# The closing rows of a gated mixer kernel: one fused scale moved to the end, one sum moved to a DMA, the order of the last operations rewritten

## The chip, the cores and the metric

The kernel runs on one core of one Trainium2 chip. The time is device microseconds of one execution; runs are given by their median. "The profile" is one execution taken by the hardware profiler, and its span runs from its first to its last instruction. The engines are PE (matmuls), ACT (ScalarE), DVE (VectorE), POOL (GpSimd) and SP (SyncE, which here only issues transfers).

## The reference

Two branches work on the same input `x = A_q` (2048 tokens of 640 values), and a gate mixes them. Branch A multiplies a shifted, weighted `k` with `v`, convolves the result along the tokens with a 2048-tap filter per channel (by Fourier transforms), adds `kv * ssm_D` and multiplies with `q`. Branch B is a layer norm, a product with `w1`, gelu, a shift of channel groups along the tokens, a product with `w2`, a residual, a second layer norm and an MLP with 1536 hidden values.

```python
x = A_q
g = _sigmoid((x * gate_w).sum(-1, keepdims=True))
...
kv = k_shift * v
y_f = kv_f * kf_f[None, :, :, :]
y = irfft2(y_f, ...)[:, 0, :S, :]
y = y + kv * ssm_D[None, None, :]
a = q * y
...
x1 = x + hs
b = x1 + _gelu(_layernorm(x1) @ w3) @ w4
return g * a + (1 - g) * b
```

## The kernel before

All tiles lie in one SBUF tensor, `arena`, and all accumulators in one PSUM tensor, `PS`, used as four pairs of banks. Tokens are split into two halves of the sequence (`c` = 0, 1), each half into 128 partitions of eight neighbours; "row" `rho` (0 to 7) is one of the eight, so that a row is 2 x 128 tokens. Channels are worked on in two halves of 320 (`half` = 0, 1).

The tile `X` first holds the input, then branch B's running result; branch B ends by leaving `(1 - g) * b` in it. Branch A runs over each half of the channels: forward transforms of the taps `h` and of `kv` by matmuls (L1178; evicted from PSUM by ACT at L694), twiddles and pointwise products on DVE (L663, a helper that issues every elementwise operation), and an inverse transform by matmuls in `inverse` (L1366 and L1341). The taps of one half give two spectra, one for each of two interleaved sets of frequencies, evicted to the slots `s3` and `s4`; the DVE work on `s3` is first.

`inverse` goes over the rows in the order `INV` = 0, 4, 2, 6, 1, 5, 3, 7. Of the second half of the channels (`half` 1), which ends the kernel, the rows 0, 4, 2 and 6 are worked whole: 8 matmuls (L1366), two ACT evictions that scale by the gate `g` (320 wide, one for each `c`), a DVE multiply with `q` (640 wide) and a DVE add into `X` (640 wide), and an output transfer of 160 KB issued by SP (L1400). The rows 1, 5, 3 and 7, at the places 4 to 7 of `INV`, are cut into pieces "a" (`c` = 0) and "b" (`c` = 1), so that "6b" is the second half of the row at place 6: 4 matmuls (L1341), one eviction, a DVE multiply and a DVE add of 320. Both pieces of a row go out in one transfer (L1359), those of place 7 each in its own (80 KB, L1356). One piece, 7b, has no ACT eviction: one DVE operation reads PSUM and does scale and multiply (L1351).

In `half` 0 a DVE multiply writes the product over `q`, and a DMA issued by POOL (L1392, queue q0) adds it into `X`; there are four such sums, each of two rows (320 KB), and SP issues the outputs behind them.

The program is recorded as nodes with costs. A planner (`_forward`) then sets each engine's order: among the nodes that are ready it takes the one that can start first by its own estimates, and the table `RANK` (one number for a node) breaks ties. It also gives out the PSUM pairs. Each engine then runs its list in that order and waits on semaphores. SP's list is such a queue too: a transfer that waits holds all that stand behind it.

Of the kernel before, what the change touches and what calls it, by code (L numbers as in the profile page):

```python
# [4 lines left out]
ENGS = ("pe", "act", "dve", "pool", "sp")  # L5
# [83 lines left out]
class Prog:  # L89
# [110 lines left out]
    def _forward(self):  # L200
# [6 lines left out]
            j.pair = None  # L207
            j.left = len(j.evicts) if j.evicts else 1
        free = {"pe": 1.0, "act": 0.7, "dve": 0.8, "pool": 1.1, "sp": 0.7}
        ready = {e: [] for e in ENGS}  # L210
        known_at = {}
        pair_free = [0.0] * PAIRS
        pair_job = [None] * PAIRS
# [11 lines left out]
        def arrive(n):  # L225
            at = 0.0
            for d in n.deps:
                t = d.end + (LAT[d.eng][0 if d.eng == n.eng else 1] if d.kind == "c" else 0.05)
                if t > at:
                    at = t  # L230
            known_at[n] = at
            ready[n.eng].append(n)

        for n in nodes:
            if n.missing == 0:
# [4 lines left out]
        while left:  # L240
            best = None
            for e in ENGS:
                for n in ready[e]:
                    t = max(known_at[n], free[e])
                    if n.first:
                        j = n.job
                        tp = None
                        for i in range(PAIRS):
                            if pair_job[i] is not None and pair_job[i].left:
                                continue  # L250
                            if j.seeded and not (bits[i][0] and bits[i][1]):
                                continue
                            if tp is None or pair_free[i] < tp:
                                tp = pair_free[i]
                        if tp is None:
                            continue
                        t = max(t, tp)
                        ok = True
                        for d in j.ext:
                            if d.end is None:  # L260
                                ok = False
                                break
                            if not n.seed:
                                t = max(t, d.end - n.cost)
                        if ok and n.seed:
                            for d in n.soft:
                                if d.end is None:
                                    ok = False
                                    break
                                t = max(t, d.end - self.LOOK)  # L270
                        if not ok:
                            continue
                    key = (t, -n.prio, n.idx)
                    if best is None or key < best[0]:
                        best = (key, n)
            assert best is not None, "schedule is stuck"
            n = best[1]
            e = n.eng
            t = best[0][0]
            ready[e].remove(n)  # L280
            n.start = t
            cost = n.cost
            if n.array:
# [153 lines left out]
def _bf16_bits(a):  # L437
# [21 lines left out]
XQ = {(0, 0): "act", (0, 1): "act"}  # L459
FIN2 = {0: 4, 1: 0}  # L460
FIN_DMA = (0,)
FIN1_DMA = 0
SEED2 = (0, 1, 2, 3, 4, 5, 6, 7)
SEED4 = (0, 1, 2, 3, 4, 5, 6, 7)
RANK = [
# [40 lines left out]
]  # L506


# [42 lines left out]
def bass_gated_mix__ssm_conv_h3__mixer_s_mlp__prompt_kernel(  # L551
# [761 lines left out]
    def inverse(half, slot0, slot1, Qh, temp):  # L1313
# [8 lines left out]
        for rho in order:  # L1322
# [63 lines left out]
                sel = slice(rho, rho + 1)  # L1386
            xs = X[:, :, sel, hs]
            n = 1280 if pair else 640
            if half in FIN_DMA or (half == 1 and order.index(rho) // 2 < FIN1_DMA):
                qs = Qh[:, :, sel, :]  # L1390
                tt(qs, g2, qs, ALU.mult, n, tag="fin")
                P.dma("pool", lambda e, ps, xs=xs, qs=qs: e.dma_start(xs, qs, accum_op=ALU.add), r=[xs, qs], w=[xs],  # L1392
# [57 lines left out]
```

## Time and profile before

| | |
|---|---|
| three runs | 225.64, 225.78, 226.91 us; median 225.78 us |
| the profiled execution | 225.55 us, its span 223.5 us |
| busy in the span | PE 216.3 us, DVE 208.7, ACT 174.6, POOL 41.1 |
| transfers | 34.04 MB, mean 152 GB/s |
| clock granted to PE | 0.998 of full speed |

The span is shorter than the time of its execution by 2.05 us, which lie around it. PE's busy time is 97% of the span, so there is little slack in the middle; what the change rewrites lies in the last 12 us.

### The profile page before, as it was taken

The numbers are of one execution on the slowest core, as the hardware profiler recorded it, in microseconds if no ns is written. First come the engines' busy times: TensorE is split into PE (matmuls) and PEld (weight loads), VectorE is DVE, ScalarE is ACT, GpSimd is POOL, SyncE is SP. The second block draws the span as 40 slices with busy tenths as digits, with TensorE's granted clock in tenths as the row PEclk, the third lists the DMA queues.
The fourth block names the chain that finished last, engine by engine and source line by source line (L and its number), as shares of the span: only waits on it lengthen the run. The fifth ranks groups of instructions, "written<-read, shape, count | busy, mean of one in ns | idle before, by whom it ended". The sixth has DMA issues, their size and how long they took to land.

```text
span 223.5 us, 3945 instructions
## 1 busy us (share of the span) xinstructions
PE 216.3 (97%) x1557; PEld 138.0 (62%) x1569; DVE 208.7 (93%) x267; ACT 174.6 (78%) x292; POOL 41.1 (18%) x48
## 2 busy tenths in 40 slices
PE   7999999999999999999999999999999999999993
PEld 7589655557676655457744455667745675577772
DVE  4999899999999899999899999799998999999976
ACT  3989999899999999999987488997145723572484
POOL 1335662403003120450200200000020002033020
PEclk9999999999999999999999999999999999999999
DMA  6999996589801968061654150003559000648667
GB/s 208 385 403 387 350 361 236 116 156 283 349 5 33 345 120 337 4 117 41 126 101 90 24 97 0 1 3 98 137 87 257 11 0 3 117 87 117 151 117 235
DMA packets 36713, 34.04 MB, mean 152 GB/s; under 512 B 17508, under 2 KB 31719, under 8 KB 36568
## 3 DMA queue, kind: packets, MB, share of 16 engines
q1 hardware_dynamic: 31560, 23.97, 35.8%
q0 software_dynamic: 4848, 9.50, 18.9%
q10 hardware_dynamic: 288, 0.33, 0.6%
q8 instruction: 12, 0.20, 0.4%
q14 instruction: 5, 0.04, 0.1%
HBM read 21.47 MB, written 3.93 MB: 114 GB/s over the span
## 4 chain that ended last, share of the span: by engine, by line
PE 76%; ACT 18%; DVE 2%; DMA 2%; issue 1%; SPq 0%; ACTq 0%
PE PS L1147 23%; PE PS L1129 23%; ACT arena L694 12%; PE PS L1178 9%; PE PS L967 8%; PE PS L1366 6%; ACT PS L1057 5%; PE PS L927 2%; ACT arena L680 2%; DVE arena L663 2%; DMA arena<-in_A_q_dram 2%; PE PS L823 1%; PE PS L769 1%; PE PS L758 1%; PE PS L780 0%
## 5 line engine op out<-in xcount | busy, mean ns | idle before, releaser
L663 DVE TENSOR_TENSOR arena<-arena 128x2560 bf16<-128x2560 bf16 (+5 forms) x175 | 186.1, 1116 | 7.0 <-ACT arena L694 3.5
L694 ACT ACTIVATE arena<-PS 128x640 bf16<-128x640 f32 (+8 forms) x142 | 104.2, 812 | 18.9 <-PE PS L1129 14.7
L1147 PE MATMUL PS<-arena 128*128 128x320 bf16 x384 | 53.3, 299 | 0.0
L1129 PE MATMUL PS<-arena 128*128 128x512 bf16 x232 | 52.2, 379 | 0.8 <-ACT arena L694 0.5
L1147 PEld LDWEIGHTS PS<-arena 128*128 128x128 bf16 x384 | 37.4, 98 | 15.0 <-issue 0.3
L694 ACT ACTIVATE arena<-PS,arena 128x320 bf16<-128x320 f32 (+1 forms) x47 | 27.7, 626 | 24.2 <-PE PS L1147 22.2
L1129 PEld LDWEIGHTS PS<-arena 128*128 128x128 bf16 x240 | 23.3, 98 | 27.4 <-issue 0.5
L1178 PE MATMUL PS<-arena 128*128 128x320 bf16 x224 | 34.4, 300 | 0.7 <-DVE arena L906 0.6
L1178 PEld LDWEIGHTS PS<-arena 128*128 128x128 bf16 x224 | 20.8, 98 | 12.8 <-ACT arena L694 2.8
L680 ACT ACTIVATE arena<-arena 128x640 bf16<-128x640 bf16 (+2 forms) x34 | 25.8, 787 | 0.8 <-DMA arena<-in_A_q_dram 0.4
L967 PE MATMUL PS<-arena 128*128 128x512 bf16 (+1 forms) x121 | 22.9, 335 | 0.2
L1075 PE MATMUL PS<-arena 128*128 128x320 bf16 x160 | 22.6, 299 | 0.0
L1057 ACT ACTIVATE PS<-arena 128x640 f32<-128x640 bf16 x32 | 22.3, 719 | 0.2
L868 POOL TENSOR_TENSOR arena<-arena 128x4 f32<-128x4 f32 (+1 forms) x9 | 14.0, 1553 | 30.7 <-DVE arena L668 30.4
L1075 PEld LDWEIGHTS PS<-arena 128*128 128x128 bf16 x160 | 15.4, 98 | 6.7 <-ACT PS L1057 0.6
L967 PEld LDWEIGHTS PS<-arena 128*128 128x128 bf16 x125 | 11.8, 98 | 8.2 <-ACT arena L694 0.5
L702 POOL DMA_DIRECT2D arena<-arena x4 | 4.8, 1202 | 57.6 <-DVE arena L663 57.6
L888 DVE BATCH_NORM_STATS2 arena<-arena 128x6 f32<-128x320 bf16 x28 | 12.4, 477 | 2.9 <-DMA arena<-in_A_q_dram 2.8
L1366 PE MATMUL PS<-arena 128*128 128x320 bf16 x96 | 14.3, 299 | 0.0
L1007 POOL DMA_DIRECT2D arena<-arena x18 | 9.7, 545 | 12.7 <-ACT arena L694 12.7
L1366 PEld LDWEIGHTS PS<-arena 128*128 128x128 bf16 x96 | 9.2, 98 | 4.3 <-issue 0.3
L1392 POOL DMA_DIRECT2D arena<-arena x4 | 5.1, 1276 | 35.7 <-ACT arena L694 25.9
(42 smaller groups left out, 81.5 us busy)
## 6 DMA issues: line engine op xcount, KB each, us to landing
arena<-in_B_w_dram POOLq DMA_DIRECT2D x4, 960.0 KB, 8.2
arena<-in_A_k_dram SPq DMA_DIRECT2D x4, 640.0 KB, 14.3
arena<-in_A_v_dram SPq DMA_DIRECT2D x4, 640.0 KB, 14.1
arena<-arena POOLq DMA_DIRECT2D x4, 640.0 KB, 6.1
arena<-in_A_q_dram SPq DMA_DIRECT2D x4, 640.0 KB, 7.4
out_dram<-arena SPq DMA_DIRECT2D x15, 160.0 KB, 2.0
arena<-in_A_q_dram SPq DMA_DIRECT2D x6, 320.0 KB, 5.5
arena<-in_A_ssm_k_dram SPq DMA_DIRECT2D x3, 512.0 KB, 11.5
```

What stands on the lines that cost most here:

```text
L663: return dve(lambda e: e.tensor_tensor(o, a, b, op), [a, b], [o], c_tt(n), tag=tag, **kw)
L680: node = P.op("act", lambda e, ps: e.activation(o, i, func, **kw), r=r, w=[o], cost=c_act(n, naps, acc is not None, psum=False), tag=tag, ...
L694: node = P.op("act", lambda e, ps: e.activation(ov, inner(ps), func, **kw), r=r, w=[o], cost=c_act(n, len(r), acc is not None), job=job, t ...
L868: P.op("pool", lambda e, ps: e.tensor_tensor(r, v, hv, ALU.pow), r=[v, HALF], w=[r], cost=cost, tag="ln")
L888: dve(lambda e, o=o, x=x: e.bn_stats(o, x), [x], [o], 0.393, tag="bn", group=("bn", id(mv), rho, c))
L967: fns.append(lambda e, ps, b=b, c=c, lhsT=lhsT: e.matmul(bank(ps, b, 256 * n), lhsT, XT[:, c, r0:r0 + n, :], start=(c == 0), stop=(c == 4)))
L1057: P.seed(job, lambda e, ps: e.activation(two(ps, 320), x, ACTF.Copy), [X[:, c, rho, :]], c_act(640, psum=False), tag)
L1075: fns.append(lambda e, ps, hh=hh, ft=ft, lhsT=lhsT: e.matmul(bank(ps, hh, 320), lhsT, w2v[:, ft, 320 * hh:320 * hh + 320], start=False, st ...
L1129: fns.append(lambda e, ps, b=b, ft=ft, c=c, sc=sc: e.matmul(bank(ps, b, 512), w3h[ft // 6][:, c, 128 * (ft % 6):128 * (ft % 6) + 128], XT[ ...
L1147: fns.append(lambda e, ps, hh=hh, ft=ft, lhsT=lhsT: e.matmul(bank(ps, hh, 320), lhsT, w4h[ft // 6][:, ft % 6, 320 * hh:320 * hh + 320], st ...
L1178: fns.append(lambda e, ps, w=w, b=b, rhs=rhs, st=(first and n == 0), en=(n == len(ss) - 1): e.matmul(bank(ps, b, 320), w, rhs, start=st, s ...
L1366: fns.append(lambda e, ps, w=w, z=z, c=c, st=(n == 0), en=(n == len(terms) - 1): e.matmul(bank(ps, c, 320), w, z[:, c, :], start=st, stop=en))
```

## The change

Three things change in what is executed. (1) Row 6 of the second half is no longer added into `X` by DVE: the multiply writes over `q`, and a DMA on POOL's queue adds it, as in the first half. Its output, which stood first of its half in SP's queue, now stands behind those of the places 4 and 6. (2) Piece 7b, whose matmuls stood before those of row 4, is now the last on PE, its fused DVE operation and its output transfer likewise; the DVE operations of the closing pieces now alternate between the add of one piece and the multiply of another. (3) In the forward transforms of the taps of the second half, the last matmuls and eviction for `s3` change places with the next-to-last for `s4`. The planner now follows `RANK` strictly, one list an engine, instead of picking among ready nodes; the table has new numbers.

```diff
-        ready = {e: [] for e in ENGS}
+        queue = {e: sorted((n for n in nodes if n.eng == e), key=lambda n: -n.prio) for e in ENGS}
...
-            ready[n.eng].append(n)
...
-                for n in ready[e]:
+                n = queue[e][len(order[e])] if len(order[e]) < len(queue[e]) else None
+                if n in known_at:
...
-            ready[e].remove(n)
...
-FIN1_DMA = 0
+FIN1_ROWS = (6,)
...
 RANK = [
-    920, 917, 905, 923, 915, 904, 888, 870, 898, 848, 853, 801, 812, 918, 877, 913, 779, 795, 738, 866, 753, 716, 721,
+    920, 917, 905, 923, 915, 904, 889, 871, 899, 853, 858, 804, 815, 918, 877, 914, 781, 798, 741, 866, 756, 720, 724,
...
-            if half in FIN_DMA or (half == 1 and order.index(rho) // 2 < FIN1_DMA):
+            if half in FIN_DMA or (half == 1 and rho in FIN1_ROWS):
                 qs = Qh[:, :, sel, :]
                 tt(qs, g2, qs, ALU.mult, n, tag="fin")
                 P.dma("pool", lambda e, ps, xs=xs, qs=qs: e.dma_start(xs, qs, accum_op=ALU.add), r=[xs, qs], w=[xs],
                       nbytes=256 * n, cost=1.3, kind="acc", tag="fina")
```

From line 281 on, the lines of the changed kernel stand one lower: L1366 is its L1365, L663 its L662. The first place is PE's last instructions. Before, the last four rows of the list are row 4's neighbours and pieces: L1366 x24 are the rows 6, 2 and 0, L1341 x4 is piece 7b, L1366 x8 is row 4, and L1341 x28 are the seven other pieces.

```order
L1366 MATMUL PS<-arena 128x320 x16
L1147 MATMUL PS<-arena 128x320 x24
L1366 MATMUL PS<-arena 128x320 x24
L1341 MATMUL PS<-arena 128x320 x4
L1366 MATMUL PS<-arena 128x320 x8
L1341 MATMUL PS<-arena 128x320 x28
```

Changed:

```order
L1365 MATMUL PS<-arena 128x320 x16
L1146 MATMUL PS<-arena 128x320 x24
L1365 MATMUL PS<-arena 128x320 x32
L1340 MATMUL PS<-arena 128x320 x32
L1419 UNCONDITIONAL_BRANCH
```

Row 4 now follows row 0 at once, and all eight pieces stand behind it, 7b last. The number of matmuls is the same.

The second place is DVE's end. A row of 640 in one run (128x640) is a multiply of a whole row, 128x2x320 an add of a whole row into `X`, 128x320 an operation of a piece. Before:

```order
L663 TENSOR_TENSOR arena<-arena 128x640
L663 TENSOR_TENSOR arena<-arena 128x2x320
L663 TENSOR_TENSOR arena<-arena 128x640
L663 TENSOR_TENSOR arena<-arena 128x2x320
L1351 SCALAR_TENSOR_TENSOR arena<-PS,arena 128x320
L663 TENSOR_TENSOR arena<-arena 128x640
L663 TENSOR_TENSOR arena<-arena 128x320
L663 TENSOR_TENSOR arena<-arena 128x2x320
L663 TENSOR_TENSOR arena<-arena 128x640
L663 TENSOR_TENSOR arena<-arena 128x320
L663 TENSOR_TENSOR arena<-arena 128x2x320
L663 TENSOR_TENSOR arena<-arena 128x320 x13
```

Changed:

```order
L662 TENSOR_TENSOR arena<-arena 128x2x320
L662 TENSOR_TENSOR arena<-arena 128x640
L662 TENSOR_TENSOR arena<-arena 128x2x320
L662 TENSOR_TENSOR arena<-arena 128x640
L662 TENSOR_TENSOR arena<-arena 128x2x320
L662 TENSOR_TENSOR arena<-arena 128x640
L662 TENSOR_TENSOR arena<-arena 128x320
L662 TENSOR_TENSOR arena<-arena 128x2x320
L662 TENSOR_TENSOR arena<-arena 128x320 x12
L1350 SCALAR_TENSOR_TENSOR arena<-PS,arena 128x320
L662 TENSOR_TENSOR arena<-arena 128x320 x2
```

The first row here is row 6's multiply, which now writes over `q` (hence its other shape). Its add is gone; the fused operation of 7b and its add have moved to the end, the fused one between the multiply and the add of 7a.

The third place is SP's queue of outputs: L1400 are whole rows, L1359 the rows at the places 4, 6 and 5, L1356 the pieces 7b and 7a. Before:

```order
L1400 DMA out_dram<-arena 128x2x320 x9
L1356 DMA out_dram<-arena 128x320
L1400 DMA out_dram<-arena 128x2x320 x3
L1359 DMA out_dram<-arena 128x2x320 x3
L1356 DMA out_dram<-arena 128x320
```

Changed:

```order
L1399 DMA out_dram<-arena 128x2x320 x11
L1358 DMA out_dram<-arena 128x2x320 x2
L1399 DMA out_dram<-arena 128x2x320
L1358 DMA out_dram<-arena 128x2x320
L1355 DMA out_dram<-arena 128x320 x2
```

The L1399 between the L1358 is row 6's output, which waits for its sum by DMA. POOL's list has one more transfer at its end (L1391, 128x2x320), that sum, behind the last sum of the first half.

76 rows, old and new, of the table RANK are left out of this document.

## The prediction

> **What bounds the kernel now.** I read the page first, then the chain of waits over the last 19 us, then the timeline of each engine there, then the transfers.
>
> ```profile
> PE 216.3 (97%) x1557; PEld 138.0 (62%) x1569; DVE 208.7 (93%) x267; ACT 174.6 (78%) x292; POOL 41.1 (18%) x48
> PE 76%; ACT 18%; DVE 2%; DMA 2%; issue 1%; SPq 0%; ACTq 0%
> ```
>
> PE is the bound: 216.3 us busy in a span of 223.5, and 76% of the chain. DVE is busy for 93% but is 2% of the chain, so most of what it gains or loses is absorbed. The change leaves PE's work as it is, so what counts is what comes after the last matmul. The end of the chain (start, length, what):
>
> ```profile
> 211.10 3.26 PE PS L1366 x24
> 214.37 0.54 PE PS L1341 x4
> 214.91 1.10 PE PS L1366 x8
> ...
> 216.03 0.95 ACT arena L694 x2
> 216.99 0.02 issue
> 217.01 3.98 DVE arena L663 x15
> ...
> 221.02 0.33 DVE arena L663
> ```
>
> PE carries the chain to 216.01 (the rows 6, 2, 0, then piece 7b, then row 4), two ACT evictions of row 4 to 216.98, and then DVE, without a pause, to 221.35. Behind it stands only the last output. The same stretch by engine (idle before the group in brackets):
>
> ```profile
> 212.48 1.26 POOL L1392 DMA_DIRECT2D arena<-arena  x1 [7.42 <-DVE arena L663]
> 213.37 1.95 DVE L663 TENSOR_TENSOR arena<-arena 128x640 bf16<-128x640 bf16 x4 [1.18 <-ACT arena L694]
> ...
> 215.23 0.54 DVE L1351 SCALAR_TENSOR_TENSOR arena<-PS,arena 128x320 bf16<-128x320 f32 x1
> 215.69 1.12 DVE L663 TENSOR_TENSOR arena<-arena 128x640 bf16<-128x640 bf16 x3
> ...
> 215.83 3.97 PE L1341 MATMUL PS<-arena 128*128 128x320 bf16 x28
> 216.03 4.33 ACT L694 ACTIVATE arena<-PS,arena 128x320 bf16<-128x320 f32 x9 [0.68 <-PE PS L1366]
> 217.01 4.33 DVE L663 TENSOR_TENSOR arena<-arena 128x640 bf16<-128x640 bf16 x16 [0.20 <-ACT arena L694]
> ```
>
> PE ends at 219.80, ACT at 220.36, DVE at 221.34. Before 217.01 DVE waits for ACT (1.18 and 0.20 us); after it DVE is the bound. SP's queue, from the release of the last DMA sum of the first half on:
>
> ```profile
> 217.05 0.37 SPq L1400 DMA_DIRECT2D out_dram<-arena  x1
> 217.47 0.47 SPq L1356 DMA_DIRECT2D out_dram<-arena  x1
> 217.99 1.51 SPq L1400 DMA_DIRECT2D out_dram<-arena  x3
> 219.54 1.61 SPq L1359 DMA_DIRECT2D out_dram<-arena  x3
> 221.37 0.34 SPq L1356 DMA_DIRECT2D out_dram<-arena  x1
> ```
>
> Nine outputs go out here, the first five steps at (219.54 - 217.05) / 5 = 0.50 us each. These do not wait for data: DVE had finished with the rows and with 7b some tenths or more before each. So SP is within a hair of being the bound as well; only the last issues wait for DVE. The windows (length, busy time of PE, PEld, DVE, ACT, POOL with counts, clock, share of the DMA engines, GB/s) say the same of the transfers:
>
> ```profile
> 214.30:216.50 2.20, 2.20 (x18) 1.57 (x17) 2.17 (x7) 1.42 (x4) 0.00 (x0) 1.00 1.22 149
> 216.50:217.50 1.00, 1.00 (x10) 0.72 (x8) 0.80 (x3) 1.00 (x4) 0.00 (x0) 1.00 1.07 322
> 217.50:218.00 0.50, 0.50 (x5) 0.35 (x4) 0.50 (x3) 0.50 (x2) 0.00 (x0) 1.00 0.09 28
> 218.00:219.00 1.00, 1.00 (x10) 0.73 (x8) 1.00 (x5) 0.92 (x3) 0.00 (x0) 1.00 0.78 245
> 219.00:222.50 3.50, 0.80 (x6) 0.35 (x4) 2.31 (x10) 1.35 (x3) 0.00 (x0) 1.00 0.97 300
> ```
>
> From 219.0 to 222.5 the DMA engines are full. Three things thus end within some tenths of each other: DVE's list, SP's list and the transfers.
>
> **The change part by part.** *PE, 0.* The matmuls are the same. Row 4 moves up by the 4 matmuls of 7b, 0.54 us, and ends at 216.01 - 0.54 = 215.47; the list still ends at 219.80, now with 7b. A wait for a PSUM pair could open a gap, but each pair's eviction lies at least 0.4 us ahead of the matmuls that take it.
>
> *ACT, 0.* The same operations. Row 4's second eviction ends at 216.98 - 0.54 = 216.44; each later piece comes 0.54 us earlier with its matmuls, 7a's ending near 219.8. None is last.
>
> *DVE, +0.05.* Row 6's add leaves (a whole-row operation), but it ran before 217.01, where DVE waits for ACT anyway: worth nothing at the end. The closing run starts 0.54 earlier, at 216.47. It takes in what 7b did before it:
>
> ```profile
> 219.02 0.79 DVE L663 TENSOR_TENSOR arena<-arena 128x320 bf16<-128x320 bf16 x3
> ```
>
> Three operations of 320 in 0.79, each 0.32 long, start every 0.24. The fused one at 215.23 is followed at 215.69: 0.46. So 0.46 + 0.24 = 0.70 is added. Alternating takes out the one pause left, between 7a's multiply and its add (0.32 + 0.04 instead of 0.24): -0.12. The run ends at 216.47 + 4.33 + 0.70 - 0.12 = 221.38, against 221.34. 7b moved from a place where DVE had time to one where it has none, and that eats the earlier start.
>
> *POOL and the sum by DMA, 0 if it lands by 220.1.* The issue stands behind the one at 212.48 (free at 213.75) and behind row 6's multiply (213.37 + 0.49). I take 214.3 to leave POOL half a microsecond. Nearest landings, from issue, in us (KB each before it):
>
> ```profile
> arena<-arena POOLq DMA_DIRECT2D x1, 320.0 KB, 4.6
> arena<-arena POOLq DMA_DIRECT2D x1, 320.0 KB, 6.3
> arena<-arena POOLq DMA_DIRECT2D x1, 640.0 KB, 6.6
> ```
>
> The first is the one at 212.48, the second that of 203.79, the third a pointwise sum at 163.36. The 320 KB hold the DMA engines for 2.2 us (the window 214.30 to 216.50), so these 160 KB hold them for 1.1, behind the others: 216.5 to 217.6, landing about 218.1. Bounds: 218.1 and 214.3 + 6.6 = 220.9. Those 1.1 us fall into the window 216.5 to 217.5, from which row 6's output (some 0.5 us) leaves; the gap at 217.5 to 218.0 takes the rest.
>
> *SP, +0.25.* This is where I expect the change to show. Row 6's output leaves the idle time at 214.4 and joins the crowd: ten outputs from 217.05 on instead of nine. At 0.50 a step the tenth starts at 217.05 + 9 x 0.50 = 221.55; the ninth (7a) waits for its add until 221.18, and one step more gives 221.68. I take 221.65, against 221.37 now, although 7b's data are there at 221.42. Bounds: 221.42 (SP keeps up; +0.05) and 221.68 plus 0.2 if a step in the full queue stretches (+0.5). The transfers agree: eight outputs of 160 KB at 0.53 and two of 80 KB from 218.0 on end near 222.8, now near 222.5.
>
> *The last landing, +0.05.* 80 KB take, from issue:
>
> ```profile
> out_dram<-arena SPq DMA_DIRECT2D x1, 80.0 KB, 1.6
> out_dram<-arena SPq DMA_DIRECT2D x1, 80.0 KB, 1.7
> ```
>
> 1.6 is the last one now, 1.7 the one inside the crowd (217.47). The new last one stands right behind another: between the two. Bounds 0 and +0.1.
>
> *The exchanged evictions, 0.* DVE waits in the middle for the last eviction of the taps' first spectrum:
>
> ```profile
> 143.63 1.49 DVE L663 TENSOR_TENSOR arena<-arena 128x2560 bf16<-128x2560 bf16 x1 [1.65 <-ACT arena L694]
> ```
>
> The evictions around it, by line and shape, and then all that PE waits for from 140 us to the end:
>
> ```profile
> L694 ACT ACTIVATE arena<-PS 128x640 bf16<-128x640 f32 x7 | 4.3, 735 | 0.0
> ```
>
> ```profile
> PEld PS L1178 <- ACT arena L694: 0.6, 3, 0.2
> PEld PS L1366 <- issue: 0.3, 1, 0.3
> PEld PS L1366 <- ACT arena L694: 0.2, 1, 0.2
> ```
>
> That eviction, one of a run of seven, now comes one place earlier, 4.3 / 7 = 0.6 us, so DVE starts its work on the second half 0.6 earlier. But PE does not wait for DVE in that time, and DVE's lead is lost at the 1.18 us wait at 213.37. If that cover were gone it would be worth up to -0.6.
>
> *Sum:* 0 + 0 + SP's 0.25 to 0.3 (DVE's 0.05 lies inside it) + 0.05 = **+0.3 us**: span 223.8, this execution 225.55 to 225.85. The median of the runs lies 0.23 above the profiled execution, so I forecast 225.78 + 0.3 = 226.1. A measurement of this kernel tells about 1% (2.3 us) from no change, so this is "the same".
>
> **The rivals.** *A late sum holds SP's queue (slower).* The outputs of place 5, 7a and 7b stand behind row 6's output, which waits for the sum. It decides from 220.1 on, when SP comes to it: each 0.1 later is 0.1 more. Landing after 6.6 us means 220.9, last issue 222.5, +0.85 over the forecast: 227.0. For it: two of the three rows above took over 6 us. Against: the 6.3 fell into outputs already moving beside it, and the nearest in place and time took 4.6 at twice the bytes. To be slower by 1% it would have to land 7.7 us after its issue.
>
> The Trainium skill speaks for this rival (SBUF — State Buffer, "SBUF: two separate sides"): while DVE runs an operation in a two-port mode, GpSimd is locked out of the shared ports and cannot write the descriptors of its DMAs. By that rule the issue would stretch while DVE works. The rows do not bear it out:
>
> ```profile
> 199.36 2.96 DVE L663 TENSOR_TENSOR arena<-arena 128x1280 bf16<-128x1280 bf16 x3
> 200.48 1.28 POOL L1392 DMA_DIRECT2D arena<-arena  x1 [2.37 <-DVE arena L663]
> ```
>
> With DVE busy throughout, the issue took 1.28; at 212.48, with DVE idle up to 213.37, 1.26. Had the descriptors to wait for the end of DVE's run at 221.38, the sum would land 4.6 - 1.26 = 3.3 later, at 224.7, and the last output would start 1.5 after that: 4.5 us more than forecast, 230.6. I give that 0.02 of this rival's 0.10.
>
> *The close is free.* SP steps faster than 0.50 when the queue of data, not of issues, is the limit, and 7b goes out at 221.42: +0.05, 225.8. For it: an issue with nothing before it takes 0.37. Against: six steps in a row at 0.5.
>
> *The exchange pays.* DVE's 0.6 reaches the end through some transfer that starts earlier: 226.1 - 0.6 = 225.5. Against: the sum that SP waits for until 217.05 is issued behind an ACT eviction that PE paces, not behind DVE.
>
> **How the numbers follow.** Forecast 0.68, free close 0.14, exchange 0.08, late sum 0.10. Run to run the times spread by 0.14 us below and 1.13 above their median, and the bounds of SP's term are +0.05 and +0.5; with the exchange below and the late sum above, the range is 225.5 to 227.0. Faster by over 1% has no case (0.02 for what I have not seen); slower by over 1% needs a landing beyond 7.7 us (0.04); the same 0.94.
>
> **What would show it.** PE's last matmul ends near 219.8 and DVE's closing run starts near 216.5, ending near 221.4: else the DVE term is wrong. SP issues ten outputs from 217.05 on, the last near 221.65: if it issues at 221.4, SP's step is wrong. Row 6's sum lands near 218.1; if SP waits for POOL's DMA after 220, the late sum is right. DVE's wait near 143 shrinks from 1.65 to about 1.05 with nothing else moving. The forecast is wrong if the span ends below 223.4 or above 224.6.

## The result: 0.2 to 0.4% longer, and the profile after

Before, 225.9 us (median of 20 runs beside the changed kernel); after, 226.72 us (226.13 to 228.54, 20 runs). The ratio is 1.0036 [1.0020, 1.0053]: about 0.8 us longer, clear of no change by its interval, and a third of the 1% that the prediction counts as the same. Measured again beside the experiments, the unaltered changed kernel took 226.4 us against 226.12: 1.0022 [0.9992, 1.0052], which does not exclude no change. The ratios leave out the few executions that were over 1.5% longer (of the profiled ones only that of the kernel with row 4 by DMA, span 228.3 us, granted clock 0.978), and are not always the quotient of the two medians.

The first profiled execution of the changed kernel took 227.75 us with a span of 225.5, 2 us longer than before's. Most of that is not the change. From the page:

```profile
PE 216.9 (96%) x1557; PEld 137.7 (61%) x1569; DVE 208.5 (92%) x266; ACT 174.8 (78%) x292; POOL 42.4 (19%) x49
L1365 PE MATMUL PS<-arena 128*128 128x320 bf16 x96 | 14.2, 299 | 0.6 <-DVE arena L662 0.6
```

DVE has one operation less and POOL one more, as the change says. The second row shows a wait of PE for DVE, 0.6 us, that before did not have. It stands at 212.40. Earlier in this execution the pointwise sum of the middle landed 8.1 us after its issue, and DVE waited 2.11 us for it; before, it landed after 6.6, and DVE waited 0.62. The rows of this transfer, of after and then of the second profile of the same kernel:

```profile
arena<-arena POOLq DMA_DIRECT2D x1, 640.0 KB, 8.1
```

```profile
arena<-arena POOLq DMA_DIRECT2D x1, 640.0 KB, 6.7
```

With 6.7 the second profile has no such wait of PE. How far an execution is set back ahead of the end is read from single matmuls. From the 801st to the end of the last one PE took 118.62 us before, 118.62 in the second profile of the changed kernel, and 118.62 or 118.63 in all the experiments below; only the first profile has 119.34. What else differs between executions lies ahead of the 801st matmul, which started between 101.1 and 105.6 us after the span's start, in kernels whose engines' lists are the same there. So single spans cannot be compared to tenths here, and everything below is counted **from the end of PE's last matmul** (219.80 before; 216.74 + 4.51 = 221.25 after). The chain of after near its end:

```profile
213.91 3.00 PE PS L1365 x22
216.92 0.02 issue
216.94 0.96 ACT arena L693 x2
217.90 0.02 issue
217.92 3.97 DVE arena L662 x15
```

Row 4 now goes straight from PE (216.92) over two evictions to DVE's closing run at 217.92, 3.33 us ahead of PE's end; before, it was 219.80 - 217.01 = 2.79. The groups of PE and of DVE, with the fused operation of 7b (L1350) inside the run and no pause around it:

```profile
216.74 4.51 PE L1340 MATMUL PS<-arena 128*128 128x320 bf16 x32
215.75 6.14 DVE L662 TENSOR_TENSOR arena<-arena 128x640 bf16<-128x640 bf16 x19 [0.42 <-ACT arena L693]
221.81 0.55 DVE L1350 SCALAR_TENSOR_TENSOR arena<-PS,arena 128x320 bf16<-128x320 f32 x1
222.27 0.55 DVE L662 TENSOR_TENSOR arena<-arena 128x320 bf16<-128x320 bf16 x2
```

DVE ends at 222.82, 1.57 after PE; before 1.54. What comes later is SP's queue. Its rows in the second profile of the changed kernel (PE's end there is 219.75, nearly before's, so that the times can be read against those of the prediction):

```profile
215.29 3.70 SPq L1399 DMA_DIRECT2D out_dram<-arena  x5
219.04 1.04 SPq L1358 DMA_DIRECT2D out_dram<-arena  x2
220.12 0.50 SPq L1399 DMA_DIRECT2D out_dram<-arena  x1
220.66 0.50 SPq L1358 DMA_DIRECT2D out_dram<-arena  x1
221.21 0.99 SPq L1355 DMA_DIRECT2D out_dram<-arena  x2
221.74 0.45 SPq L1355 DMA_DIRECT2D out_dram<-arena  x1
```

(The last row is the second of the two in the row before, by itself.) 7b's result is there at 219.75 + 1.57 = 221.32, and its output is issued at 221.74. From 219.04 to 221.74 SP takes five steps of 0.54. From the release of the last sum of the first half (216.99 here, 218.58 in the first profile) to the last of the ten issues it is 4.75 and 4.77 us; before, with nine, it was 221.37 - 217.05 = 4.32. The windows of the same execution:

```profile
214.90:217.00 2.10, 2.10 (x17) 1.50 (x16) 1.93 (x5) 1.96 (x5) 0.38 (x1) 1.00 1.21 148
217.00:217.50 0.50, 0.50 (x6) 0.38 (x4) 0.50 (x3) 0.50 (x2) 0.00 (x0) 1.00 1.26 214
217.50:218.00 0.50, 0.50 (x6) 0.35 (x5) 0.50 (x4) 0.50 (x2) 0.00 (x0) 1.00 1.19 243
218.00:219.00 1.00, 1.00 (x9) 0.73 (x8) 1.00 (x6) 0.92 (x3) 0.00 (x0) 1.00 1.10 336
219.00:222.50 3.50, 0.75 (x6) 0.30 (x4) 2.32 (x9) 0.76 (x2) 0.00 (x0) 0.98 1.00 309
```

The share of the DMA engines is 1.00 or more from 214.9 to 222.5 without a break; before, the window 217.50 to 218.00 stood at 0.09. The last piece of data landed 1.70 after its issue, and the span ended 0.48 after that.

The tails, in us after PE's last matmul (last result of DVE, last issue of an output, last landing, end of the span), with the times. The first six rows carry the argument; the others come below. Each tail is that of one execution.

| kernel | DVE | issue | landing | span | median, before beside it | ratio |
|---|---|---|---|---|---|---|
| before | 1.54 | 1.57 | 3.19 | 3.68 | 225.9 | |
| after, first profile | 1.57 | 2.10 | 3.80 | 4.29 | 226.72, 225.9 | 1.0036 [1.0020, 1.0053] |
| after, second profile | 1.57 | 1.99 | 3.69 | 4.17 | 226.4, 226.12 | 1.0022 [0.9992, 1.0052] |
| before + row 6's sum by DMA | 1.54 | 1.95 | 3.71 | 4.19 | 226.47, 225.96 | 1.0025 [0.9998, 1.0052] |
| before + 7b last, alternating | 1.57 | 1.75 | 3.43 | 3.92 | 226.06, 225.96 | 1.0003 [0.9980, 1.0025] |
| before + exchanged evictions | 1.54 | 1.57 | 3.20 | 3.69 | 226.24, 225.96 | 1.0000 [0.9973, 1.0027] |
| after, two outputs issued by ACT | 1.57 | 1.60 | 3.70 | 4.18 | 226.38, 225.98 | 1.0028 [1.0010, 1.0046] |
| after, last sum of the first half on DVE | 1.56 | 1.80 | 3.51 | 4.00 | 226.2, 225.96 | 0.9999 [0.9974, 1.0023] |
| before, last sum of the first half on DVE | 1.54 | 1.57 | 3.21 | 3.69 | 226.02, 225.98 | 1.0005 [0.9989, 1.0021] |
| three closing adds on POOL | 2.65 | 2.86 | 4.56 | 5.05 | 227.22, 225.98 | 1.0060 [1.0037, 1.0083] |
| row 4 by DMA in place of row 6 | 1.54 | 1.57 | 3.56 | 4.09 | 227.23, 225.98 | 1.0037 [1.0015, 1.0059] |
| DVE's close trimmed, 7a's output by ACT | 1.42 | 1.45 | 3.38 | 4.16 | 226.63, 226.12 | 1.0031 [1.0007, 1.0055] |

The tail grew by 0.61 in one profile of the changed kernel and 0.49 in the other. Both lie inside what the medians show: 0.5 us of 225.9 is a ratio of 1.0022, 0.6 is 1.0027.

### The profile page after: what moved, and what is told of

The parts are those of the page before. It is cut to its first block, busy times and chain, and to the rows that moved or that the text cites. A ratio compares the mean times of both kernels' runs of the same rounds, so it can differ in the third digit from the quotient of the medians.

```text
span 225.5 us, 3945 instructions
## 1 busy us (share of the span) xinstructions
PE 216.9 (96%) x1557; PEld 137.7 (61%) x1569; DVE 208.5 (92%) x266; ACT 174.8 (78%) x292; POOL 42.4 (19%) x49
## 4 chain that ended last, share of the span: by engine, by line
PE 41%; DVE 24%; ACT 22%; DMA 10%; SPq 1%; issue 1%; DVEq 0%
DVE arena L662 23%; ACT arena L693 15%; PE PS L1128 15%; PE PS L966 7%; PE PS L1177 7%; DMA arena<-arena 6%; PE PS L1146 6%; ACT PS L1056 5%; DMA arena<-in_A_q_dram 3%; PE PS L1365 2%; PE PS L926 2%; ACT arena L679 2%; PE PS L822 1%; SPq L705 1%; DVE arena L887 1%
## 5 line engine op out<-in xcount | busy, mean ns | idle before, releaser
L662 DVE TENSOR_TENSOR arena<-arena 128x2560 bf16<-128x2560 bf16 (+5 forms) x174 | 185.9, 1119 | 8.3 <-ACT arena L693 3.1
L701 POOL DMA_DIRECT2D arena<-arena x4 | 4.8, 1204 | 59.1 <-DVE arena L662 59.1
L1365 PE MATMUL PS<-arena 128*128 128x320 bf16 x96 | 14.2, 299 | 0.6 <-DVE arena L662 0.6
L1391 POOL DMA_DIRECT2D arena<-arena x5 | 6.3, 1252 | 35.3 <-ACT arena L693 23.8
L1006 POOL DMA_DIRECT2D arena<-arena x18 | 10.1, 568 | 12.0 <-ACT arena L693 11.9
L1365 PEld LDWEIGHTS PS<-arena 128*128 128x128 bf16 x96 | 9.2, 98 | 5.0 <-issue 1.1
```

What stands on the lines that cost most here:

```text
L662: return dve(lambda e: e.tensor_tensor(o, a, b, op), [a, b], [o], c_tt(n), tag=tag, **kw)
L1365: fns.append(lambda e, ps, w=w, z=z, c=c, st=(n == 0), en=(n == len(terms) - 1): e.matmul(bank(ps, c, 320), w, z[:, c, :], start=st, stop=en))
```

## The experiments

All of them use the strict lists of the changed planner, with numbers written for each.

**The three parts of the change, each alone on the kernel before.** First row 6's sum by DMA. The fused piece stays ahead of row 4.

```diff
-FIN1_DMA = 0
+FIN1_ROWS = (6,)
 # DVE: row 6's add leaves; POOL: its sum last; PE, ACT: as before
 # SP: row 6's output behind those of the places 4 and 6; 7b's where it was
```

> The kernel before, with one part of the change alone: row 6 is added by DMA and its output stands behind those of the places 4 and 6; all else as before. Theory Q (the queue of outputs): the ten transfers that SP issues after the last sum of the first half at some 0.53 us a step set the end. Here there are ten again, so most of the change's cost appears: last issue 4.7 to 4.8 us after that release (4.32 before), +0.4 to +0.6 us on the median. Theory D (the fused operation of 7b at DVE's end costs): 7b is in its old place, so no cost, 0 or -0.1 us. Theory M (the exchange in the middle moves the DMA sums there): 0.

The tail was 4.19, as long as with all three parts together. SP's last rows (PE's end here is 222.27):

```profile
222.03 1.05 SPq L1359 DMA_DIRECT2D out_dram<-arena  x2
223.13 0.50 SPq L1400 DMA_DIRECT2D out_dram<-arena  x1
223.67 0.51 SPq L1359 DMA_DIRECT2D out_dram<-arena  x1
224.22 0.49 SPq L1356 DMA_DIRECT2D out_dram<-arena  x1
```

DVE ended at 222.27 + 1.54 = 223.81, and the last output went out at 224.22: 0.41 late, with the same operations in DVE's closing run. The release of the last sum of the first half came at 219.52, so the ten issues took 4.70, as theory Q expected. This part alone makes the tail 0.51 longer.

Second, 7b last and the closing operations alternating, while row 6 keeps its DVE add and its early output.

```diff
 # PE:  row 6, 2, 0, then
-#      7b, row 4, the seven other pieces
+#      row 4, the seven other pieces, 7b
 # DVE: the fused operation of 7b between 7a's multiply and add
 # SP:  7b's output last
```

> The kernel before, with the second part alone: piece 7b is last on PE, its fused operation and output last, DVE's closing operations alternate; row 6 is added by DVE and goes out first, as before. Theory Q: nine transfers after the release, the last one issued when DVE is done (some 0.05 later than before) or one step of 0.53 after 7a's: +0.1 us, at most +0.3. Theory D: +0.5 to +0.8 us. Theory M: 0.

The last two rows of SP's queue here (PE's end 221.26), the second being the last output by itself:

```profile
222.62 0.82 SPq L1356 DMA_DIRECT2D out_dram<-arena  x2
223.01 0.43 SPq L1356 DMA_DIRECT2D out_dram<-arena  x1
```

DVE ends at 222.83 and 7b's output starts at 223.01, since 7a's went out only 0.39 before. DVE's work costs 0.03, about as predicted, but the second 80 KB output right behind the first costs 0.18 at the issue, and the tail grows by 0.24.

Third, the two evictions of the taps exchanged.

```diff
 # PE, ACT (taps, second half of the channels)
-#   ... last of s3, next-to-last of s4
+#   ... next-to-last of s4, last of s3
```

> The kernel before, with the third part alone: the last evictions of the two spectra of the taps change places. Theory Q and D: 0 on the median (within 0.2 us); DVE's wait near 143 us shrinks from 1.65 to about 1.1 us, and the gain is gone at a later wait of DVE. Theory M: +0.3 us or more, with a DMA sum of the middle (the ones issued near 163 and 197) landing later than in the kernel before.

DVE in the middle, here:

```profile
144.84 5.96 DVE L663 TENSOR_TENSOR arena<-arena 128x2560 bf16<-128x2560 bf16 x6 [1.14 <-ACT arena L694]
151.62 0.83 DVE L663 TENSOR_TENSOR arena<-arena 128x1280 bf16<-128x1280 bf16 x1 [0.82 <-ACT arena L694]
```

The wait shrinks from 1.65 to 1.14, and the next wait for ACT, six operations on, grows from the 0.23 of before to 0.82: the lead is gone 7 us after it was won. Tail +0.01, ratio 1.0000. The parts add up to 0.51 + 0.24 + 0.01 = 0.76, more than the 0.49 to 0.61 of the whole: where row 6's output keeps SP's queue full, moving 7b's output to its end hardly matters, for the ten issues take 4.70 without it and 4.75 to 4.77 with it.

**Is SP slow at issuing, or are the DMA engines full?** Two of the changed kernel's late outputs, row 6's and 7a's, go out on ACT's queue.

```diff
-P.dma("sp", ... d=dst[:, c, :] ...)
+P.dma("sp" if c else "act", ... d=dst[:, c, :] ...)
...
-P.dma("sp", ... src=src, dst=dst ...)
+P.dma("act" if half == 1 and r1 == 6 else "sp", ... src=src, dst=dst ...)
```

> The changed kernel, with two of its ten closing outputs (row 6 and 7a) issued by ACT, which has nothing left to do by then, instead of SP. The bytes and the order in which data come are the same. Theory S (the time that one issue takes on SP is the limit): eight outputs on SP, the last issue when DVE is done, 1.6 us after the last matmul instead of 2.10, end 3.8 us after it instead of 4.29; 0.4 to 0.5 us faster than the changed kernel. Theory E (the DMA engines are the limit, and SP's step of 0.54 is their pace): the outputs are issued earlier and land as late as before, end 4.2 to 4.3 us after the last matmul, no gain over the changed kernel.

The timeline (PE's end 219.82), the window and the last two landings:

```profile
221.42 0.34 SPq L1356 DMA_DIRECT2D out_dram<-arena  x1
219.32 0.41 ACTq L1400 DMA_DIRECT2D out_dram<-arena  x1
221.19 0.36 ACTq L1356 DMA_DIRECT2D out_dram<-arena  x1
```

```profile
219.00:222.50 3.50, 0.82 (x7) 0.37 (x4) 2.39 (x10) 0.83 (x2) 0.00 (x0) 1.00 1.08 331
```

```profile
out_dram<-arena ACTq DMA_DIRECT2D x1, 80.0 KB, 2.0
out_dram<-arena SPq DMA_DIRECT2D x1, 80.0 KB, 2.1
```

7b's output was issued 1.60 after PE's end, 0.4 to 0.5 earlier than in the changed kernel and as soon as its data were there. It landed at 3.70, as before that edit: 2.10 after its issue instead of 1.70. By the end of the span theory E is right. The Trainium skill states a rule that fits (DMA: Bandwidth & Descriptors, "Issuing engines are not separate DMA queues"): transfers issued from several engines run on the same 16 DMA engines, and only the issuing time is saved. For the last landing this run agrees, and not even that time was saved.

But the run does not show that the DMA engines were at their limit. The trace records the landing of an output in sixteen steps, as many as there are DMA engines. Fifteen of 7b's had come by 3.36 here and by 3.66 in the second profile of the changed kernel, so for them the earlier issue was worth 0.30; the sixteenth alone, 0.34 behind the others, made the 3.70. In the changed kernel the last step was late as well, by up to 0.2 until 7a's output, but by only 0.03 at 7b's. Why it is late is open. The window moved 331 GB/s where the changed kernel moved 309, so a share of 1.00 was not the most that the engines could carry. The medians cannot decide: 1.0028 here, 1.0036 and 1.0022 for the unaltered changed kernel, and the intervals are wider than 0.4 us.

Nor is SP's step of 0.54 shown to be the pace of the transfers. In the kernel before, SP took steps of 0.50 to 0.52 from 217.47 to 219.00, while the windows 217.50 to 218.00 and 218.00 to 219.00 stood at 0.09 and 0.78, so at most 0.04 of the 0.54 goes with full DMA engines. An issue with none right before it on its queue took 0.34 even where they were full (the first row above). And in the changed kernel the step behind 7a's 80 KB is 0.53, as behind 160 KB. The two limits lie close together, for 160 KB (163,840 bytes) at the 309 GB/s of the window are 0.53; which of them holds the last output back is not separated here.

**Less in the crowd.** The last sum of the first half of the channels (the rows 3 and 7) is added by DVE, which waits there anyway, in the changed kernel and in the kernel before. Its two outputs then leave ahead of the crowd.

```diff
+if half == 0 and rho == 7:
+    tt(xs, xs, qs, ALU.add, n, tag="finv")
+else:
     P.dma("pool", ... accum_op=ALU.add ...)
```

> The changed kernel, with the last sum of the first half (rows 3 and 7) added by DVE in place of a DMA, and its two outputs issued before those of the second half. SP is then not held until the landing of that sum. Theory Q: its eight closing outputs go out as their data come, 7b's right after DVE's last add instead of 0.75 us after it; 0.5 to 0.8 us faster than the changed kernel, thus about the time of the kernel before (-0.1 to +0.2 us). Theory D: no gain over the changed kernel (+0.5 to +0.8 us over before). Theory M: no gain.

```profile
220.42 0.50 SPq L1403 DMA_DIRECT2D out_dram<-arena  x1
220.97 0.50 SPq L1359 DMA_DIRECT2D out_dram<-arena  x1
221.59 0.90 SPq L1356 DMA_DIRECT2D out_dram<-arena  x2
222.04 0.46 SPq L1356 DMA_DIRECT2D out_dram<-arena  x1
```

SP now waits for 7a's data (221.59 comes 0.62 after 220.97), and the tail is 4.00, 0.17 to 0.29 shorter than in the changed kernel, not the 0.5 to 0.8 expected. 7b's output still goes out 0.24 after DVE's last add, one step behind 7a's. By the ratio (0.9999) the changed kernel's loss is gone, by the medians 0.24 us of it is left, and the interval is as wide as the loss. What is left in the tail against before, 0.32, is for the most part the pair of 80 KB outputs, which cost 0.24 in the run of the second part alone.

> The kernel before, with the last sum of the first half (rows 3 and 7) added by DVE instead of a DMA and its two outputs issued ahead. SP has no crowd then. Theory Q (SP's outputs set the end where there are ten, DVE where there are nine): DVE sets the end here already, so 0 on the end (3.6 to 3.7 us after the last matmul, as before), though the outputs of the crowd go out up to 1 us earlier. Were SP's queue the bound of the kernel before too: 0.2 to 0.4 us faster than before.

In the kernel before, the same edit moved nothing: 3.69 against 3.68, ratio 1.0005. There DVE's list sets the last issue, and room in SP's queue and in the transfers is worth nothing.

**Shorter closing work on DVE.** With the transfers relieved, DVE's list is what is left. Three of its closing adds go to POOL (row 6's add on DVE again, last sum on DVE).

```diff
+ON_POOL = ((6, 1), (4, 1), (4, 0))
...
+if (at, c) in ON_POOL:
+    P.op("pool", lambda e, ps, x=x, t=t: e.tensor_tensor(x, x, t, ALU.add), ...)
+else:
     tt(x, x, t, ALU.add, 320, tag="finl")
```

> The order of the changed kernel, with row 6 added by DVE, the last sum of the first half added by DVE, and three adds of the pieces 6b, 4b and 4a done by POOL instead of DVE, so that DVE's closing run is 0.7 us shorter. Nearest row for one such add on POOL: 0.96 us (one partition, 320 elements). Theory Q: with no crowd at SP and DVE's list shorter, 7b's fused operation starts when its matmuls end, last issue about 1.0 to 1.2 us after the last matmul (1.57 before), end 3.1 to 3.3 after it instead of 3.68: 0.4 to 0.5 us faster than before. Rival: POOL and DVE hold each other up, the adds take 2 us or more each, and the outputs of the places 4 and 6 hold SP's queue: slower than before by 1 us or more.

The groups by line and shape from 216.9 to 223, then the same groups of the changed kernel (second profile, 216.4 to 221.4):

```profile
L664 DVE TENSOR_TENSOR arena<-arena 128x320 bf16<-128x320 bf16 x12 | 4.9, 464 | 0.0
L1356 POOL TENSOR_TENSOR arena<-arena 128x320 bf16<-128x320 bf16 x3 | 2.6, 876 | 12.5 <-DVE arena L664 12.5
```

```profile
L662 DVE TENSOR_TENSOR arena<-arena 128x320 bf16<-128x320 bf16 x15 | 3.8, 319 | 0.0
```

DVE has three operations less and takes 1.1 us longer: on average 464 ns for each instead of 319. The average hides two kinds. Nine took 0.31 to 0.33 us as ever, and three, one beside each add on POOL, took 0.91. The first such pair:

```profile
217.97 0.91 DVE L664 TENSOR_TENSOR arena<-arena 128x320 bf16<-128x320 bf16 x1
217.74 0.96 POOL L1356 TENSOR_TENSOR arena<-arena 128x320 bf16<-128x320 bf16 x1 [12.24 <-DVE arena L664]
```

DVE's operation ended at 218.88, 0.18 after POOL's, and so did the other two. Three times 0.59 more and three operations of 0.24 less are the 1.1 us by which DVE ends later. The tail is 5.05, the clearest loss of all. The rival was right that DVE is held up, and in the size (1.4 us in the tail), though an add on POOL took 0.80 to 0.96, not 2 us; whether DVE also holds POOL up is not shown, as the nearest row of an add on POOL, of another shape, has 0.96. The Trainium skill has the mechanism (SBUF — State Buffer, "SBUF: two separate sides"): a DVE operation with two inputs in SBUF shares a pair of ports with a GpSimd operation that reads SBUF, and whichever comes first has it for a whole instruction. The run agrees: each of the three operations of DVE lasted until POOL's had ended.

A DMA issue on POOL is another matter. Beside DVE's run from 215.75 on, the issue of row 6's sum in the first profile of the changed kernel took no longer than the 1.26 of the one at 212.48 before:

```profile
215.62 1.18 POOL L1391 DMA_DIRECT2D arena<-arena  x1 [0.34 <-DVE arena L662]
```

**Another row by DMA.** Row 4, whose add stands in DVE's closing run, is summed by DMA in place of row 6; last sum on DVE, 7a's output on ACT.

```diff
-FIN1_ROWS = (6,)
+FIN1_ROWS = (4,)
 # SP: row 4's output behind place 5's
```

> The order of the changed kernel, but row 4 (whose add lies in DVE's closing run) is added by DMA instead of row 6, the last sum of the first half is added by DVE in its idle time, row 4's output stands behind that of place 5, and 7a's output is issued by ACT. Theory Q: DVE ends 1.15 us after the last matmul instead of 1.57, row 4's sum lands 3.2 us after its issue, about 0.9 after the last matmul, and the last issue is 1.2 to 1.3 after it, end 3.35 to 3.45 instead of 3.68: 0.2 to 0.3 us faster than before, 0.8 to 0.9 faster than the changed kernel. Rival: the sum lands late (4.6 us after its issue), row 4's output then holds 7b's, last issue 2.6 us after the last matmul, end about 4.7: 1 us slower than before.

The expectation missed: DVE ended at 1.54, as before. The eviction of 7a and the multiply that reads it, here (PE's end is 224.21), and then the same eviction in the second profile of the changed kernel (PE's end 219.75):

```profile
223.70 0.53 ACT L694 ACTIVATE arena<-PS,arena 128x320 bf16<-128x320 f32 x1
224.26 0.33 DVE L663 TENSOR_TENSOR arena<-arena 128x320 bf16<-128x320 bf16 x1
```

```profile
219.25 0.53 ACT L693 ACTIVATE arena<-PS,arena 128x320 bf16<-128x320 f32 x1
```

7a's eviction starts 0.5 before PE's end in both, for it follows 7a's matmuls, and 7b's 0.54 us of matmuls come after them. The multiply starts 0.06 after PE's end here and 0.08 after it in the changed kernel, with the same work behind it. So DVE's shorter list came up against ACT's evictions, which start at the same times from PE's end in the two kernels: three of DVE's steps, to 221.71, 223.24 and 224.26, took 0.42, 0.35 and 0.30 instead of 0.24, 0.36 more together, where the add had taken 0.40. Row 4's sum landed 3.2 after its issue and held nobody. The last three outputs went out within 0.5 us, and the last one landed 1.99 after its issue. The tail's 0.41 lies inside the interval of the ratio.

**The changed kernel once more**, unaltered, for the size of the tail and of the middle:

> The changed kernel again, unaltered, for a second profile of it. If the crowd of outputs is the cause, its close repeats whatever the middle does: last issue 2.05 to 2.15 us after the last matmul, end 4.25 to 4.35 after it (3.68 in the kernel before), and the median is +0.5 to +0.9 over before. If the wait of PE for DVE that its first profile shows (0.56 us) were part of the change, it shows again; if it came from one late DMA sum of that execution, it doesn't.

It gave a tail of 4.17 against 4.29, a last issue at 1.99 and a median 0.3 above before: each below what was expected, and the wait of PE did not come back. The last sum of the first half landed 2.67 ahead of PE's end in the first profile and 2.76 in the second, which is most of the difference in the last issue; from that landing on the two closes agree (4.77 and 4.75).

**The close trimmed.** On the kernel before: last sum on DVE, 7a's multiply ahead of 5a's add, and 7a's output on ACT.

```diff
 # DVE, closing run
-#  ... 5a add, 7a multiply, 7a add
+#  ... 7a multiply, 5a add, 7a add
-P.dma("sp", ... d=dst[:, c, :] ...)
+P.dma("sp" if c else "act", ... d=dst[:, c, :] ...)
```

> The kernel before, with the last sum of the first half added by DVE in its idle time (its two outputs ahead), the multiply of 7a ahead of the add of 5a, and 7a's output issued by ACT. DVE's list sets the end of the kernel before, so only its pause can go: DVE ends 1.43 us after the last matmul instead of 1.54, end 3.55 to 3.6 after it instead of 3.68; -0.1 us on the median, within the noise of the runs. Were SP or the DMA engines still the limit: 3.3 or less.

```profile
217.18 4.21 DVE L663 TENSOR_TENSOR arena<-arena 128x640 bf16<-128x640 bf16 x16 [0.20 <-ACT arena L694]
221.42 0.35 ACTq L1356 DMA_DIRECT2D out_dram<-arena  x1
out_dram<-arena ACTq DMA_DIRECT2D x1, 80.0 KB, 1.9
```

DVE's run lost its pause (4.33 to 4.21), as the prediction had priced it. But the expectation missed: the last output landed at 3.38, 1.93 after its issue. 5a's add now comes second, so the output of place 5 was issued 1.21 after PE's end instead of 0.97, only 0.24 ahead of 7a's instead of 0.60, and the last landing followed its landing by 0.26. Then the span ended 0.78 after the last landing instead of the 0.48 to 0.54 of the other tails: 4.16, longer than before, ratio 1.0031. The trace puts that 0.3 on ACT, whose queue landed last here: its last DRAIN instruction begins 0.40 after the end of the branch ahead of it, where SP's in the kernel before begins 0.14 after. Why is open; with two outputs on ACT above, ACT's began 0.13 after, and the last landing was SP's. No version beat the kernel before.

## Why the prediction was right in kind and short in size

The forecast was 226.1 us, the same within 1%, inside 225.5 to 227.0. Measured: 226.72, and 226.4 the second time. As a difference, it was +0.3; the runs gave +0.8 (interval 0.45 to 1.2) and +0.3 (-0.2 to 1.2), the tails +0.61 and +0.49. That the second median agrees is no proof, as wide as its interval is; by the tails the forecast was 0.2 to 0.3 short. The mechanism it named, SP's output queue taking over from DVE at the end, is what happened: the last output waited 0.42 to 0.53 for SP and not for its data. The span of 223.9 in the second profile lies inside the 223.4 to 224.6 that the prediction set as its sign; the 225.5 of the first lies outside, for the reasons ahead of the tail that were told above. The third part of the change, which lies near 143 us and not in the last 12, added nothing.

- **PE and ACT, 0:** right; 118.62 us from the 801st matmul to the last, before and in the second profile after.
- **DVE, +0.05:** right; +0.03 (1.54 to 1.57). The closing run started 3.33 ahead of PE's end; forecast was 219.80 - 216.47 = 3.33.
- **SP, +0.25 to 0.3:** mis-sized, and the one term that was. It took 0.50 for SP's step, the mean of five steps from 217.05 on, of which the first was 0.42 and one was an 80 KB output's. In the full crowd a step was 0.54, and the last issue came 0.42 later in one profile and 0.53 in the other. The upper bound given, +0.5, was the right end. The rows of before would have given it: SP's steps from 219.00 to 220.08 were 0.54, and 217.05 + 0.42 + 8 x 0.54 = 221.79; measured was 221.74 with PE ending 0.05 earlier. The prediction also took from the share of 0.97 that the DMA engines were full. The run with two outputs on ACT moved more in the same window (331 against 300 GB/s), so that is not shown.
- **The last landing, +0.05:** 1.70 after its issue instead of 1.62: +0.08.
- **The sum by DMA:** forecast to land at 218.1, it landed at 214.11 + 4.49 = 218.60 in the second profile, 4.57 after its issue in the first. SP came to row 6's output at 220.12, so nobody waited: the late sum was not the rival that decided. Its bytes filled the gap at 217.5 to 218.0 and ran beside the outputs up to 218.6; what that cost is not separated.
- **The exchange, 0:** right in size; 1.65 to 1.14 (forecast 1.05). But the lead was lost at the next wait for ACT, by 149.8, and not at 213.37 as the prediction had it.

Of the rivals, "the close is free" needed a last issue at 221.42; it came at 221.74 with PE ending 0.05 earlier. "The exchange pays" found nothing in its own run: tail +0.01, ratio 1.0000. The case in which DVE's run holds back the sum's descriptors (230.6) did not occur: the issue took 1.18 beside DVE's run in both profiles. Its condition, a two-port mode, is one that no run shows DVE's operations here to be in. As to which part costs: row 6's sum by DMA, 0.51 of the tail alone, since it takes an output out of idle time at 214.4 and makes it one more in a row of issues back to back; 7b last, 0.24 alone. No run puts row 6's output late without its sum. That the place of the output costs, and not the sum's bytes, is argued from SP's steps after the first, which were 0.50 to 0.55 in that run and 0.50 to 0.54 in the kernel before. Whether the medians' 0.3 to 0.8 hold anything beside the tail's 0.5 to 0.6 cannot be told within their intervals.

## What to carry to other kernels

Where a kernel ends in a row of outputs, count the issues of the queue from its last release on, at the step that the trace shows for issues back to back (0.54 us here), and hold against it the bytes of an output over the rate of that window (0.53 us for 160 KB here). Where the two are equal, relieving one alone may not move the end. An operation taken from a vector engine ahead of a wait buys nothing: DVE ended at 1.54 with and without row 6's add. An output that leaves while the queue is idle should stay there, even if a vector engine has to add for it. Where runs differ by 2 us at the start, count the tail from the last instruction that all versions share.

## What was not expected of the hardware

- A vector add on POOL (0.80 to 0.96 us) held up one operation of DVE beside it until 0.18 us after its own end: 0.91 us instead of 0.32. The others kept their time.
- A DMA sum of 160 KB landed 4.5 us after its issue behind another sum, and 3.2 us without one ahead of it. From the kernel with the last sum on DVE:

```profile
arena<-arena POOLq DMA_DIRECT2D x1, 160.0 KB, 3.2
```

- An output issued 0.4 to 0.5 earlier landed no earlier (2.10 after its issue instead of 1.70), because the last of the sixteen steps of its landing came 0.34 behind the others; the other fifteen came 0.30 earlier than in the changed kernel.
